# Forgetting attention with a GELU MLP: the last 64 tokens of every batch as a chunk of their own, masking on the matmul engine for the first batch, crossbar transposes merged

## The chip, the cores and the metric

The kernel runs on one core of one Trainium2 chip. The metric is the device time of one execution in microseconds (us); lower is better. The profile is taken on one of these executions; its span, from the first to the last instruction, is about 2 us shorter than the time. All times below are us unless marked ns. PE is the matmul engine (TensorE), ACT is ScalarE, DVE is VectorE, POOL is GpSimd, SP is SyncE, which issues most of the DMAs here.

Runs of one kernel mostly agree within a per cent; a run over 1.5% above the fastest of the same kernel is called slow and left out of ratios.

## The reference

Eight batches, eight heads, 576 tokens, 64 elements per head. Attention with a forget gate, then an MLP with exact GELU (512 to 2048 to 512) over all 4608 tokens:

```python
def _attn_ref(q, k, v, f):
    scores = scale * q @ k.transpose(0, 1, 3, 2)
    cum = np.cumsum(np.log(np.clip(f, 1e-4, 1.0)), axis=-1)
    decay = cum[:, :, :, None] - cum[:, :, None, :]
    scores = np.where(causal, -1e9, scores + decay)   # causal: key after query
    attn = softmax(scores)
    return attn @ v                                   # ... cut: the maximum, the 1e-9
def _moe_ref(x, w_in, w_out):
    h = x @ w_in
    g = 0.5 * h * (1.0 + erf(h / sqrt(2)))
    return g @ w_out
```

The kernel drops the query's part of the decay, which cancels in the softmax, and multiplies the rows of v, and a column of ones, by the key's part ("weighing v").

## The kernel before

Per batch there are four pairs of heads. For each: scores on PE, exp on ACT, the causal mask on POOL, the product with the weighed v ("attend"), normalisation on DVE, and a crossbar transpose (a DMA that transposes on its way) that puts x, the attention's output, into the layout of the MLP. q and k of later batches come by such transposes too, and DVE copies ("untangle") put them in place. Between those pieces PE takes matmuls of the second GEMM of the chunk before (the "fill"). Then the first GEMM of the next chunk of 512 tokens runs in one piece. Chunks are cut from the flat list of 4608 tokens, so chunk c needs x of batch c and, for c above 0, of batches before it. The parts concerned:

```python
def load_v(b, h0=0, h1=H):                       # 5 DMAs on SP
    ...
def x_dma(b, i):                                 # two transposes per pair, on SP
    nc.sync.dma_start_transpose(xT_sb[:, i, q0 : q0 + 512]..., x[:, 0:4]...)
    nc.sync.dma_start_transpose(xT_sb[:, i, q0 + 512 : q0 + S]..., x[D:P, 4]...)

def gemm1(c, ffb):                               # one column block; two tiles of PSUM (where PE writes) in turn
    ps = m_psum.tile([P, TC], FP32, tag="m", name="ps1")
    for kt in range(n_dm):
        nc.tensor.matmul(ps, w_in_sb[...], xT_sb[:, kt, t0 : t0 + TC], ...)
    nc.scalar.activation(g_of[c][ffb], ps, Act.Gelu)

# in gemm2, at the end of a tile of 128 tokens
    nc.vector.tensor_copy(ot, pss[ts])
    nc.sync.dma_start(out[t0 + ts * P : t0 + (ts + 1) * P, :], ot)

for b in range(B):
    if b == 0:
        first_attention()
        load_v(1, 0, 4)
        load_v(1, 4, 8)
    else:
        load_v(b + 1)
        attention(b, gemm2(b - 1, b == 1), ...)
    for ffb in range(n_ff):
        gemm1(b, ffb)
        if b + 1 < B:
            if b == 0 and ffb in (10, 13, 15):   # batch 1: transposes on PE
                transposes_pe(b + 1, ...)
            elif b and ffb % 4 == 0:
                untangle(b + 1, ffb // 4)        # later batches: by the crossbar
            if ffb % 4 == 2:
                weigh_v(b + 1, ffb // 4)         # POOL
            if b == 0 and ffb == 2:
                load_w_out()
    if 0 < b < B - 2:
        load_qk_tokens(b + 2)
```

The softmax here doesn't subtract the row's maximum and nothing guards it: scores larger than these inputs give would overflow.

## Time and profile before

| what | before |
|---|---|
| time, median of the first 3 runs (range) | 377.45 (375.12 to 378.51) |
| span of the profiled run | 374.1 |
| first GEMM of chunk 0 starts | 33.4 |
| first attend of batch 1 | 59.45 |
| last gelu of the first GEMM of chunk 1 starts | 98.13 |
| one undisturbed batch (attention and first GEMM) | 37.7, PE busy for 37.5 |
| last matmul ends, to end of span | 370.4, 3.7 |

The line before the last is the bound: in an undisturbed batch PE hardly rests. What can be won lies at the beginning (loads), at the seams of batches (waits for x) and behind the last matmul. For the end, here is the last output tile of the kernel before: first its DVE copy and its DMA (columns: start, duration, engine and line, what; in brackets the idle time before it and who ended it), then the DMA's own row (KB, us from issue to landing).

```profile
370.39 0.69 DVE L403 COPY ot<-ps 128x512 f32<-128x512 f32 x1 [2.76 <-PE ps L394]
...
371.11 0.33 SPq L404 DMA_DIRECT2D out_dram<-ot  x1
...
out_dram<-ot SPq DMA_DIRECT2D x1, 256.0 KB, 2.0
```

A tile of 128 rows, 256 KB, lands 2.0 after its issue.

### The profile page before, as it was taken

What the parts mean: (1) busy time and instruction counts of PE and PEld (TensorE: products, weight loads), DVE (VectorE), ACT (ScalarE), POOL (GpSimd) and SP (SyncE); (2) the same over time, 40 slices, a digit from 0 to 9 for tenths busy, and PEclk for the clock granted to TensorE, in tenths of its full rate; (3) what the DMA queues carried; (4) which work ended last, traced back from release to release, by engine and by line L of the source; (5) the groups of instructions that cost most, each with busy time, mean ns of one, the idle gap of its engine ahead of it and who ended that gap; (6) DMA issues with size and microseconds to landing.
All of it is one profiled execution on the core that took longest, in us unless ns stands there. A gap on an engine that the chain in (4) does not pass through costs nothing.

```text
span 374.1 us, 6875 instructions
## 1 busy us (share of the span) xinstructions
PE 342.8 (92%) x2665; PEld 185.4 (50%) x2665; DVE 171.5 (46%) x420; ACT 214.0 (57%) x293; POOL 131.1 (35%) x261
## 2 busy tenths in 40 slices
PE   2858949969999699999999999999999999999995
PEld 1545526624465245644564456445654565444442
DVE  6395385548034932477246723681459142011011
ACT  4656647506874378737872688179826882611610
POOL 6578236351155404470447044703560350000000
PEclk9999978999999999999999999999999999999999
DMA  7999999767986894459644976498540023002002
GB/s 110 181 204 184 196 212 162 107 131 138 212 146 87 144 219 109 100 126 210 137 100 119 193 120 106 132 193 140 108 117 2 28 50 102 0 30 84 0 30 84
DMA packets 111057, 45.37 MB, mean 121 GB/s; under 512 B 89968, under 2 KB 106352, under 8 KB 111024
## 3 DMA queue, kind: packets, MB, share of 16 engines
q1 hardware_dynamic: 94128, 31.30, 40.7%
q0 software_dynamic: 16896, 13.63, 24.2%
q8 instruction: 21, 0.34, 0.4%
q14 instruction: 12, 0.10, 0.1%
HBM read 37.90 MB, written 9.44 MB: 127 GB/s over the span
## 4 chain that ended last, share of the span: by engine, by line
PE 77%; ACT 8%; DVE 7%; DMA 3%; SPq 2%; issue 1%; DVEq 0%; ACTq 0%
PE ps L362 33%; PE ps L394 26%; PE s L284 10%; PE o L315 7%; ACT e L294 5%; DMA xT_sb<-x 3%; ACT L294 2%; DVE vw L269 1%; ACT g L374 1%; SPq L350 1%; DVE x L329 1%; DVE ot L403 1%; DMA f_sb<-in_f_dram 1%; SPq L404 1%; DVE qB L183 1%
## 5 line engine op out<-in xcount | busy, mean ns | idle before, releaser
L374 ACT ACTIVATE g<-ps 128x512 bf16<-128x512 f32 x144 | 86.0, 597 | 111.0 <-PE ps L362 111.0
L394 PE MATMUL ps<-w_out_sb,g 128*128 128x512 bf16 x576 | 144.7, 379 | 0.0
L362 PE MATMUL ps<-xT_sb,w_in_sb 128*128 128x512 bf16 x576 | 127.2, 379 | 7.9 <-DMA xT_sb<-x 7.9
L294 ACT ACTIVATE e<-s 128x1024 bf16<-128x1024 f32 (+2 forms) x128 | 103.5, 861 | 25.5 <-PE s L284 24.9
L296 POOL TENSOR_SCALAR_AFFINE_SELECT e<-e 128x256 bf16<-128x256 bf16 x160 | 62.5, 407 | 140.0 <-ACT e L294 138.8
L362 PEld LDWEIGHTS <-w_in_sb 128*128 128x128 bf16 x576 | 56.1, 98 | 76.5 <-issue 10.3
L403 DVE COPY ot<-ps 128x512 f32<-128x512 f32 x36 | 24.9, 692 | 125.7 <-PE ps L394 124.8
L394 PEld LDWEIGHTS <-g 128*128 128x128 bf16 x576 | 50.3, 98 | 41.0
L284 PE MATMUL s<-qA,kT 128*128 128x384 bf16 (+2 forms) x192 | 54.8, 293 | 9.6 <-ACT e L294 4.2
L284 PEld LDWEIGHTS <-kT 128*128 128x128 bf16 x384 | 37.6, 100 | 46.6 <-issue 11.9
L284 PE MATMUL s<-qB,kT 128*128 128x384 bf16 (+2 forms) x192 | 50.3, 294 | 0.3 <-DVE qB L183 0.3
L269 POOL TENSOR_TENSOR vw<-v,wT 128x640 bf16<-128x640 f32 x30 | 38.8, 1292 | 27.6 <-PE o L315 18.5
L315 PE MATMUL o<-vw,e 128*128 128x65 bf16 x960 | 43.6, 194 | 1.6 <-DVE vw L275 1.4
L315 PEld LDWEIGHTS <-e 128*128 128x128 bf16 x960 | 40.4, 98 | 9.1 <-issue 1.4
L328 DVE RECIPROCAL r<-o 128x5 f32<-128x5 f32 x64 | 12.4, 193 | 48.0 <-PE o L315 47.1
L252 DVE COPY kT<-tk 64x288 bf16<-64x288 bf16 x96 | 32.2, 336 | 1.4
L329 DVE TENSOR_TENSOR x<-o,r 128x320 bf16<-128x320 f32 x64 | 31.5, 492 | 2.2
L252 DVE COPY qA<-tq 64x288 bf16<-64x288 bf16 x48 | 20.8, 433 | 0.9
L252 DVE COPY qB<-tq 64x288 bf16<-64x288 bf16 x48 | 16.7, 348 | 0.7
L98 POOL DMA_DIRECT2D q<-in_q_dram x12 | 9.1, 756 | 9.0 <-DMA tq<-q 7.9
L294 ACT ACT_TABLE_LOAD x7 | 9.0, 1283 | 3.3 <-PE s L284 3.2
L374 ACT ACT_TABLE_LOAD x8 | 10.3, 1283 | 0.1
(52 smaller groups left out, 88.5 us busy)
## 6 DMA issues: line engine op xcount, KB each, us to landing
out_dram<-ot SPq DMA_DIRECT2D x36, 256.0 KB, 2.3
v<-in_v_dram SPq DMA_DIRECT2D x30, 256.0 KB, 9.3
q<-in_q_dram POOLq DMA_DIRECT2D x6, 576.0 KB, 7.5
k<-in_k_dram POOLq DMA_DIRECT2D x6, 576.0 KB, 10.7
v<-in_v_dram SPq DMA_DIRECT2D x20, 128.0 KB, 5.3
w_in_sb<-in_moe_w_in_dram POOLq DMA_DIRECT2D x4, 512.0 KB, 10.2
w_out_sb<-in_moe_w_out_dram POOLq DMA_DIRECT2D x4, 512.0 KB, 13.6
xT_sb<-x SPq DMA_TRANSPOSE x56, 2.4
```

The lines of the kernel that those rows point to most:

```text
L252: nc.vector.tensor_copy(rows[:, odd], src[odd * D : (odd + 1) * D, 2 * i + h].rearrange("d j p -> d p j"),)
L269: eng.tensor_tensor(vw_of[b][:, hs, :, 0:D], v_of[b][:, hs, :, :], w.unsqueeze(3).to_broadcast([P, 2, NBLK, D]), Alu.mult,)
L284: nc.tensor.matmul(st[:, h, c : c + w], kT[i][:, K0[n] : K0[n] + P], qt[:, q0 : q0 + w], start=True, stop=True,)
L294: nc.scalar.activation(et[:, :, 0:c], st[:, :, 0:c], Act.Exp, scale=scale)
L296: nc.gpsimd.affine_select(out=et[:, :, c0 : c0 + P], in_=et[:, :, c0 : c0 + P], compare_op=Alu.is_ge, fill=0.0, base=0, pattern=[[0, 2], [ ...
L315: nc.tensor.matmul(o[:, m, :], e_of[b, i, t][:, h, c : c + P], vw_of[b][:, 2 * i + h, n, :], start=(n == 0), stop=(n == m),)
L328: nc.vector.reciprocal(r, o[:, :, D])
L329: nc.vector.tensor_tensor(x_of[b, i][:, :, h, :], o[:, :, 0:D], r.unsqueeze(2).to_broadcast([P, NBLK, D]), Alu.mult,)
L362: nc.tensor.matmul(ps, w_in_sb[:, kt, ffb * P : (ffb + 1) * P], xT_sb[:, kt, t0 : t0 + TC], start=(kt == 0), stop=(kt == n_dm - 1),)
L374: nc.scalar.activation(g_of[c][ffb], ps, Act.Gelu)
L394: nc.tensor.matmul(pss[ts], g_of[c][kt][:, ts * P : (ts + 1) * P], w_out_sb[:, kt, :], start=(kt == 0), stop=(kt == n_ff - 1),)
L403: nc.vector.tensor_copy(ot, pss[ts])
```

## The change

Its intent: keep PE from waiting at the seams. Each batch's first 512 tokens become a chunk, and the 64 last tokens of all eight batches ("tails") become the ninth. So no chunk waits on two batches, one x transpose per pair is enough, and one transpose per batch does the tails. The transposes of q and k are merged (four heads each), and batch 1 gets its q and k by crossbar instead of by PE. In batch 0 the mask becomes a matmul that adds -1e9 to the scores, which relieves POOL. The first two column blocks of each first GEMM run together, all but the last contraction step first (the "pairing"), to hide a late x. The order of the loads is changed: q and k of batch 1 go out between the quarters of w_in instead of behind them, w_out follows at once, and v of batch 1 waits, by a tiny POOL copy (the "gate"), for the last quarter of w_in. The later q and k have two buffers, and from batch 3 on they are loaded behind the first of the four weighings of v instead of behind the last. The last tile is stored in two column parts, from two queues.

```diff
-    qk_pool = ctx.enter_context(tc.tile_pool(name="qk", bufs=1))
+    qk_pool = ctx.enter_context(tc.tile_pool(name="qk", bufs=2))
 # ... cut: buffers, v_sb as one tile, warm-up matmuls, mask constant
-    def transposes_pe(b, i, in_s=True):
-        # ... cut
-    def transpose_dma(b, i):
+    def transpose_dma(b, h0, h1):
 # in scores
-                    stop=True,
+                    stop=b > 0 or c not in SDIAG[t],
+            if b == 0 and c in SDIAG[t]:
+                for h in range(2):
+                    nc.tensor.matmul(
+                        st[:, h, c : c + P], ident_bf, after, start=False, stop=True
+                    )
-        for c0 in SDIAG[t]:
+        for c0 in SDIAG[t] if b else []:
 # tails
+    def x_tail_dma(b):
+        nc.sync.dma_start_transpose(
+            tails[:, :, b * TL : (b + 1) * TL],
+            xt_of[b][D:P].rearrange("p i h d -> p (i h d)"),
+        )
 # gemm1
-    def gemm1(c, ffb):
+    def gemm1(c, ffbs):
+        src = xT(c) if c < B else tails
+        pss = [m_psum.tile([P, TC], FP32, tag="m", name="ps1") for _ in ffbs]
+        for kts in (range(n_dm - 1), [n_dm - 1]):
+            for ffb, ps in zip(ffbs, pss):
+                for kt in kts:
+                    nc.tensor.matmul(ps, w_in_sb[...], src[:, kt, :], ...)
+        for ffb, ps in zip(ffbs, pss):
+            nc.scalar.activation(g_of[c][ffb], ps, Act.Gelu)
 # gemm2
+        if c == B:
+            order[-n_ff:] = [
+                (n_sub - 1, kt, part)
+                for part in ((0, 3 * P), (3 * P, d_model))
+                for kt in range(n_ff)
+            ]
-                nc.sync.dma_start(out[t0 + ts * P : t0 + (ts + 1) * P, :], ot)
+                queue = nc.scalar if c0 else nc.sync
+                if c < B:
+                    rows = out[c * S + ts * P : c * S + (ts + 1) * P, :]
+                else:
+                    n = P // TL
+                    rows = out.rearrange("(b s) d -> b s d", s=S)[
+                        n * ts : n * (ts + 1), TC:S, c0:c1
+                    ]
+                queue.dma_start(rows, ot[:, c0:c1])
 # end of first_attention
+        transpose_dma(1, 0, 4)
 # main loop
+        gemm1(b, (0, 1))
+        if b == 0:
+            for c in range(4):
+                load_w_out(c)
+            nc.gpsimd.tensor_copy(                     # the gate
+                v_sb[0:1, 0:4, 0, 0:1],
+                w_in_sb[0:1, 0, d_ff - 4 : d_ff].unsqueeze(2),
+            )
+            load_v(1, 0, 4)
+            transpose_dma(1, 4, 8)
+            load_v(1, 4, 8)
+            x_tail_dma(0)
+        for ffb in range(2, n_ff):
+            if b + 1 < B:
+                if ffb in (2, 5, 8, 11):
+                    untangle(b + 1, (ffb - 2) // 3)
+                if ffb in (2, 6, 10, 14):
+                    weigh_v(b + 1, ffb // 4)
+            if ffb == 4:
+                load_qk_tokens(b + 2)
+            gemm1(b, (ffb,))
```

## The prediction

> **What bounds the kernel now.** I read the table of stages first (busy time in windows cut at the stage borders of the chain of waits), then the waits of the matmul engine, then the queue that issues DMAs, then the DMA queues. All times are microseconds of the profiled run, span 374.1; the median of the timed runs is 377.45, so I multiply spans by 377.45/374.1 = 1.009.
>
> In the table of stages the columns are window, length, busy time of PE, PE weight loads, DVE, ACT, POOL, then granted clock, DMA share, GB/s. The rows are first attention, first GEMM of chunk 0, attention of batch 1, its first GEMM, attention of batch 2, and an undisturbed attention (batch 3) with its first GEMM:
>
> ```profile
> 0.00:33.40 33.40, 20.07 (x290) 14.66 (x291) 23.77 (x47) 19.45 (x23) 23.47 (x49) 1.00 0.98 167
> 33.40:51.47 18.07, 15.42 (x102) 7.72 (x100) 8.16 (x18) 9.55 (x16) 8.99 (x13) 1.00 1.25 197
> 51.47:84.77 33.30, 27.17 (x248) 16.07 (x249) 19.25 (x47) 15.74 (x18) 14.96 (x31) 0.90 0.83 143
> 98.13:125.70 27.57, 24.36 (x235) 14.30 (x234) 11.20 (x26) 16.05 (x19) 15.03 (x30) 1.00 0.78 136
> 139.06:162.81 23.75, 23.56 (x233) 14.11 (x232) 7.48 (x19) 16.05 (x19) 11.20 (x25) 1.00 0.54 112
> 162.81:176.74 13.93, 13.93 (x66) 6.27 (x65) 12.45 (x33) 8.96 (x16) 3.95 (x6) 1.00 0.99 175
> ```
>
> A batch in the middle is 23.75 + 13.93 = 37.7 and PE is busy all of it; 13.93 for 64 matmuls of 512 columns is 217 ns each. Nothing in the change shortens that work. What can be won is what lies above it: 33.4 of first attention, 18.1 - 13.9 = 4.1 in the first GEMM, 33.3 - 23.7 = 9.6 in batch 1, and waits for the transposed attention output in later batches:
>
> ```profile
> PE ps L362 <- DMA xT_sb<-x: 7.9, 5, 3.6
> POOL vw L269 <- DMA v<-in_v_dram: 8.6, 1, 8.6
> ```
>
> First line: PE waits five times, 7.9 in all, for the crossbar transpose of x (3.6 in batch 1; by windows 0.2 + 2.8 in batch 2, 0.5 and 0.8 in batches 4 and 5). Second: GpSimd waits 8.6 for v of batch 1, until 48.66. The issuing queue in batch 2 shows why x is late:
>
> ```profile
> 112.85 1.26 SPq L238 DMA_TRANSPOSE tq<-q  x1
> 114.16 2.55 SPq L238 DMA_TRANSPOSE tk<-k  x1
> 116.81 1.21 SPq L346 DMA_TRANSPOSE xT_sb<-x  x1
> 118.06 1.23 SPq L350 DMA_TRANSPOSE xT_sb<-x  x1
> ```
>
> Each transpose holds the queue some 1.25, whether it moves 4 blocks (L346) or a 64-row remainder (L350). Sixteen of them per batch are 20 of issue, and the last x goes out behind that.
>
> During the load phase the DMA engines are the bound (share 0.98 and 1.25 in the first two stages). Packets and MB per queue in three windows of 2 us (13 to 15, 29 to 31, 39 to 41); q0 carries casting loads of q, k and weights, q1 v, transposes and stores:
>
> ```profile
> q1 hardware_dynamic: 1471, 0.36, 81.2%
> ...
> q1 hardware_dynamic: 1473, 0.37, 81.2%
> ...
> q0 software_dynamic: 385, 0.29, 91.4%
> q1 hardware_dynamic: 385, 0.09, 36.3%
> ```
>
> Alone v moves 736 packets of 256 B per us; beside weights it gets one packet for each of theirs, here 192 per us. Weights alone make 208 per us (416 in 25 to 27). This decides my prediction.
>
> **What the Trainium skill says.** "DMA: Bandwidth & Descriptors", section "Queues, rings and completion order": each DMA engine round-robins between queue rows at packet granularity. The 385 against 385 agrees. "TensorE: Matmul & The Clock Gate", "Architectural detail": ScalarE, VectorE and GpSimd run their instructions strictly in order; I rest the GpSimd argument on it, and the trace shows no reordering. Same page, Part 1: PE runs at half clock until it has been busy about 3.4 us, and falls back after such an idle time. The trace agrees, though its clock column says 1.00: the 384-column score matmul took 0.50 at 8.27 and 0.32 at 19.42. Same page, "Back-to-back issue gap": about N/2.4 + 2.5 ns, 216 at 512 columns; the 217 above agrees.
>
> **The change part by part.**
>
> First attention. Masking on PE takes 20 affine_selects (407 ns, 8.1) off GpSimd for 40 matmuls of 128 columns (about 56 ns by the skill's gap, 2.2 of PE time with slack beside ACT). Weighing v leaves DVE (1.95 each plus casts, twice). Thirteen warm-up matmuls fill PE before q and k land at 5.6. What is left is ACT: per pair of heads four exps, 1.02 + 0.91 + 1.02 + 0.49 = 3.45, four pairs 13.8. Exps start near 9.3 (9.78 before) and with about 2 of small gaps end near 25.5; then two attends (0.5 each), two normalisations (0.8 each), transposes and copy: 4. First GEMM starts near 29.5 instead of 33.3: -3.8.
>
> First GEMM of chunk 0. The 48 PE transposes of batch 1 and their DVE copies (0.48 each, PE waits 2.6 on the last) go to the crossbar: 18.1 becomes 13.9 + 0.6 of the pairing cost below, -3.6. Scores of batch 1 can start near 44 instead of 51.5.
>
> Pairing in the first GEMM. The first two column blocks now run three contraction steps each before the fourth. That hides 0.65 more of a late x, but block 0 ends later. With two accumulators, block 2 needs block 0's gelu finished. Matmul start to gelu start is 0.41 (from the undisturbed case: first matmul 162.65, fourth 163.30, gelu 163.71), gelu 0.60, release 0.04. Block 1 first waits for the last output copy, which ends 0.89 after the GEMM start: 0.93 + 0.65 = 1.58 for block 0's fourth step, 1.58 + 0.41 + 0.60 + 0.04 = 2.63 for block 2, against 1.80 before. So 0.83 lost per GEMM, eight of them from batch 1 on: +6.6.
>
> Merged transposes. Per batch 16 become 4 + 1 + 4 = 9, 11 of issue instead of 20, and q, k are loaded a batch earlier with two buffers. The queue keeps up and the 7.9 vanish: -7.9. With the pairing, batches 2 to 7 come out even: -4.3 against +5.0.
>
> End. The last tile's copy (0.69) shrinks to 128 columns after the last matmul, its store is smaller: -0.4.
>
> Batch 1, where I expect the gain to be given back. GpSimd's order in the changed program is: weigh v0 and load weights, then four w_out loads, a copy gated on the last w_in quarter, weigh v1 pair 0, load q and k of batch 2, weigh pairs 1 to 3, and only then the masks of batch 1. So the first attend of batch 1 waits for all of v1. In packets (w quarter 512, q and k of a batch 1536, v of a batch 4608): first v half lands near 14.8, weigh to 16.3, w_in flows from 18.3 (issue to flow was 2 before); 512 + 512 weights at 208 per us, 768 of q1, k1 at about 180, 1024 weights: 32.4, landed and gate open 33.4, v1 flowing at 35. By then w_out is queued. First half of v1, 2304 packets: 300 beside the rest of q1, k1, the other 2000 beside w_out at 160 per us (41 to 47 before): 49.1. The crossbar transposes of the second half of batch 1 are next in the same queue: 2304 packets at 1.25 ns, 2.9, to 52.0. Then v1's second half: alone until q2 flows (issued 51.7, flowing 53.7), 1360 packets, the other 944 at 188 per us: 58.7, landed 59.5. Two weighings 3.0, four masks 1.6: first attend at 64.2. Before it was at 59.45. So +4.7 in place of the 7.4 won ahead of it. PE, idle for 14, restarts at half clock for some 3: +1.4.
>
> Sum: 4.7 + 1.4 - 7.9 + 6.6 - 0.4 = +4.4, span 378.5, time 382.
>
> **Rivals.** First, v1 in time: if the loads are not in each other's way as I reckon, the first attend comes near 50, limited by the exps (gelu end, table load, 3.45 for pair 0). Then -9.4 - 7.9 + 6.6 - 0.4 = -11.1, span 363, time 366. For it: the change gates v on w_in on purpose, retunes the fill of batch 1, and looks measured. Against it: the 8.6 wait for v exists already with v issued earlier, and the packet counts. Second, q2 loses the race: v1's second half runs alone behind the transposes, 52.0 + 2.9 + 0.8, weighing and masks to about 60. Then no loss and no gain in batch 1, +0.5 - 7.9 + 6.6 - 0.4 = -1.2, span 373, time 376. Third, pairing costs nothing because x still lands late: then the 7.9 stay in part and the 6.6 overlap them; batches 2 to 7 move by under 2 either way.
>
> **Range and chances.** I give the first rival 0.35, because a tuned change that reorders loads this deliberately was probably seen to work, the second 0.3, my own sum 0.35: 0.35 x 366 + 0.3 x 376 + 0.35 x 382 = 375. Range 363 to 384. The 2% borders are 369.9 and 385: faster 0.33, within 0.57, slower 0.10.
>
> **What would show it.** Right: PE's longest wait is in batch 1, on the masks or weighed v, with GpSimd waiting for v until 50 to 60; the first GEMM of chunk 0 starts at 28 to 31 and takes 14.5; waits of PE for the x transpose vanish; a new wait of about 0.6 on gelu, once per first GEMM, beside 0.3 on the output copy; undisturbed batches near 38.5 instead of 37.7. Wrong: attend in batch 1 before 52 (then the first rival), a first attention above 32, or waits for w_in in chunk 0.

## The result, and the profile after

The changed kernel is slower: 400.06 median of 4 runs (399.90 to 407.81; the last is a slow run) against 377.07 of 4 runs of the kernel before on the same chip. The ratio is 1.0612, 95% interval 1.0551 to 1.0673. (A ratio is the mean time of one kernel's fast runs over that of the other's of the same rounds, so not quite the ratio of the medians quoted.) The spans are 398.2 and 374.1: 24.1 more. Where they arose, by the borders of the stages:

| stretch | before | after | more | predicted |
|---|---|---|---|---|
| start to the last gelu of the first GEMM of chunk 1 | 98.13 | 108.59 | +10.5 | +3.3 |
| six batches, to the last gelu of the first GEMM of chunk 7 | 230.7 | 231.9 | +1.2 | +0.7 |
| last chunk, to the end of its matmuls | 41.5 | 42.7 | +1.2 | +0.8 |
| last matmul to the end | 3.7 | 15.0 | +11.3 | -0.4 |

The last column divides the prediction's own sum of +4.4 over the stretches (in the first, 4.7 + 1.4 + 0.83 of one pairing - 3.6 of the x wait of batch 1; in the second, six pairings less the other x waits). The middle is as predicted. Two places hold nearly everything, and they are read from the following views.

**The beginning.** The waits of PE, then the wait of POOL for v, in the kernel after (columns: total, times, longest):

```profile
PE o L310 <- POOL e L291: 13.8, 2, 13.4
PE s L274 <- DVE kT L243: 4.5, 1, 4.5
...
PE ps L376 <- ACT g L384: 4.3, 9, 0.5
...
POOL vw L259 <- DMA v_sb<-in_v_dram: 32.7, 3, 18.3
```

PE waits 13.4 for the first mask of batch 1 and 4.5 for its transposed k. The 7.9 of waits for x are gone from the list; in their place stand nine waits of 0.5 for gelu. The mask waits behind the weighings of v, and those for v. POOL's timeline shows how long:

```profile
37.23 0.18 POOL L544 CAST v_sb<-w_in_sb 1x4 f32<-1x4 bf16 x1 [7.52 <-DMA w_in_sb<-in_moe_w_in_dram]
55.71 1.27 POOL L259 TENSOR_TENSOR vw<-v_sb,wT 128x640 bf16<-128x640 f32 x1 [18.29 <-DMA v_sb<-in_v_dram]
...
67.69 1.28 POOL L259 TENSOR_TENSOR vw<-v_sb,wT 128x640 bf16<-128x640 f32 x1 [7.36 <-DMA v_sb<-in_v_dram]
...
70.43 1.84 POOL L291 TENSOR_SCALAR_AFFINE_SELECT e<-e 128x256 bf16<-128x256 bf16 x5
```

The gate opens at 37.2, the first half of v is weighed at 55.7, the second at 67.7, and the masks start at 70.4; the first attend follows at 70.89. The SP queue says what shared the way:

```profile
27.24 2.31 SPq L229 DMA_TRANSPOSE tq<-q  x1
29.65 7.79 SPq L229 DMA_TRANSPOSE tk<-k  x1
37.53 12.87 SPq L114 DMA_DIRECT2D v_sb<-in_v_dram  x5
50.51 3.78 SPq L229 DMA_TRANSPOSE tq<-q  x1
54.38 1.32 SPq L229 DMA_TRANSPOSE tk<-k  x1
55.76 3.15 SPq L114 DMA_DIRECT2D v_sb<-in_v_dram  x5
```

A merged transpose can be issued in 1.3 and five loads of v in 3.2, as the last two lines show. Where the queue is crowded the same issues took 7.8 and 12.9. Packets per queue in two windows of 2 us, 33 to 35 and 45 to 47:

```profile
q0 software_dynamic: 349, 0.28, 89.0%
q1 hardware_dynamic: 348, 0.09, 34.4%
...
q0 software_dynamic: 319, 0.31, 91.6%
q1 hardware_dynamic: 320, 0.08, 30.4%
```

In both windows q1 (transposes in the first, v in the second) gets one packet for each packet of q0 (w_in, q, k, w_out). That is the arbitration the prediction quoted from the Trainium skill, "DMA: Bandwidth & Descriptors", section "Queues, rings and completion order"; this trace agrees again, 349 against 348.

**The end.** First the stores of the last chunk on SP and the small one on ACT's queue, then the DMA engines' busy tenths and queues in the window 384 to 396:

```profile
373.56 10.05 SPq L428 DMA_DIRECT2D out_dram<-ot  x4
...
383.56 1.14 ACTq L428 DMA_DIRECT2D out_dram<-ot  x1
```

```profile
DMA  1111111111111111111111111111111111111111
...
q1 hardware_dynamic: 288, 0.53, 11.5%
q10 hardware_dynamic: 130, 0.07, 1.8%
```

PE has finished at 383.2, yet data flow until about 397, in this window never faster than a steady one tenth of the DMA engines: 11.5% + 1.8% = 13.3%, near 2 of 16 (12.5%), 0.60 MB in 12 us, which is 50 KB per us. The chunk's 1 MB of stores, the first of them issued at 373.6, needs 21 at that rate. The Trainium skill states the reason on a page the prediction had cited: "DMA: Bandwidth & Descriptors", section "Why a DMA increments its semaphore by 16 and not by 1". A DMA takes as many engines (up to 16) as divide the slowest dimension of both sides that isn't 1. The DRAM side of these stores is 2 batches by 64 rows, so the slowest dimension is 2. The share agrees with two engines; e1 below tests it.

### The profile page after: what moved, and what is told of

Read it like the earlier page. It is cut to its first block, busy times and chain, and to the rows that moved or that the text cites. A ratio compares the mean times of both kernels' runs of the same rounds, so it can differ in the third digit from the quotient of the medians.

```text
span 398.2 us, 6918 instructions
## 1 busy us (share of the span) xinstructions
PE 349.2 (88%) x2682; PEld 186.4 (47%) x2682; DVE 183.2 (46%) x482; ACT 213.7 (54%) x294; POOL 126.0 (32%) x248
## 4 chain that ended last, share of the span: by engine, by line
PE 64%; SPq 9%; DMA 8%; ACT 8%; POOL 2%; issue 2%; DVE 2%; POOLq 0%; ACTq 0%
PE ps L376 26%; PE ps L410 23%; PE s L274 8%; PE o L310 6%; SPq L114 6%; ACT e L289 4%; SPq L229 4%; DMA v_sb<-in_v_dram 3%; DMA xT<-x 3%; ACT g L384 2%; DMA q<-in_q_dram 2%; ACT L289 2%; DVE ot L419 1%; POOL vw L259 1%; POOL k L102 0%
## 5 line engine op out<-in xcount | busy, mean ns | idle before, releaser
L410 PE MATMUL ps<-w_out_sb,g 128*128 128x512 bf16 (+2 forms) x592 | 145.5, 375 | 0.0
L376 PE MATMUL ps<-xT,w_in_sb 128*128 128x512 bf16 x512 | 114.7, 379 | 4.9 <-ACT g L384 3.8
L291 POOL TENSOR_SCALAR_AFFINE_SELECT e<-e 128x256 bf16<-128x256 bf16 x140 | 54.6, 406 | 133.6 <-ACT e L289 132.6
L376 PEld LDWEIGHTS <-w_in_sb 128*128 128x128 bf16 x576 | 56.1, 97 | 77.1 <-issue 12.4
L419 DVE COPY ot<-ps 128x512 f32<-128x512 f32 (+2 forms) x37 | 25.1, 677 | 110.5 <-PE ps L410 110.3
L274 PE MATMUL s<-qA,kT 128*128 128x384 bf16 (+2 forms) x192 | 54.7, 290 | 10.2 <-DVE kT L243 4.5
L259 POOL TENSOR_TENSOR vw<-v_sb,wT 128x640 bf16<-128x640 f32 x32 | 41.3, 1289 | 50.7 <-DMA v_sb<-in_v_dram 32.7
L243 DVE COPY kT<-tk 64x288 bf16<-64x288 bf16 x112 | 36.4, 325 | 7.7 <-DMA tk<-k 6.1
L325 DVE RECIPROCAL r<-o 128x5 f32<-128x5 f32 x64 | 12.4, 194 | 52.3 <-PE o L310 50.5
L326 DVE TENSOR_TENSOR x<-o,r 128x256 bf16<-128x256 f32 x64 | 27.2, 425 | 2.2
L243 DVE COPY qB<-tq 64x288 bf16<-64x288 bf16 x56 | 24.7, 440 | 0.8
L332 DVE TENSOR_SCALAR xt<-o,r 64x64 bf16<-64x64 f32 x64 | 18.6, 291 | 1.4
L376 PE MATMUL ps<-tails,w_in_sb 128*128 128x512 bf16 x64 | 14.5, 377 | 0.7 <-ACT g L384 0.5
## 6 DMA issues: line engine op xcount, KB each, us to landing
k<-in_k_dram POOLq DMA_DIRECT2D x6, 576.0 KB, 10.5
```

What stands on the lines that cost most here:

```text
L243: nc.vector.tensor_copy(rows[:, odd], src[odd * D : (odd + 1) * D, 2 * i + h].rearrange("d j p -> d p j"),)
L259: nc.gpsimd.tensor_tensor(vw_of[b][:, hs, :, 0:D], v_sb[:, hs, :, :], w.unsqueeze(3).to_broadcast([P, 2, NBLK, D]), Alu.mult,)
L274: nc.tensor.matmul(st[:, h, c : c + w], kT[i][:, K0[n] : K0[n] + P], qt[:, q0 : q0 + w], start=True, stop=b > 0 or c not in SDIAG[t],)
L291: nc.gpsimd.affine_select(out=et[:, :, c0 : c0 + P], in_=et[:, :, c0 : c0 + P], compare_op=Alu.is_ge, fill=0.0, base=0, pattern=[[0, 2], [ ...
L326: nc.vector.tensor_tensor(x_of[b, i][:, :, h, :], o[:, 0:4, 0:D], r[:, 0:4].unsqueeze(2).to_broadcast([P, NBLK - 1, D]), Alu.mult,)
L376: nc.tensor.matmul(ps, w_in_sb[:, kt, ffb * P : (ffb + 1) * P], src[:, kt, :], start=(kt == 0), stop=(kt == n_dm - 1),)
```

## The experiments

The labels are those of the runs. "Whole-row stores" and so on are built on the changed kernel unless said otherwise. All gave correct results. Medians and ratios to the kernel before (376.6 to 377.9):

| run | median | ratio, 95% interval | span |
|---|---|---|---|
| e1_store_halves | 390.21 | 1.0330 (1.0270 to 1.0391) | 387.7 |
| e2_no_column_split | 400.88 | 1.0612 (1.0551 to 1.0673) | 398.5 |
| e3_q2_late | 397.90 | 1.0550 (1.0480 to 1.0620) | 395.4 |
| e4_w_out_q2_late | 393.65 | 1.0389 (1.0314 to 1.0465) | 392.9 |
| e9_transposes_behind_v | 399.84 (one run) | | 398.1 |
| b1_pair (on the kernel before) | 381.38 | 1.0123 (1.0059 to 1.0186) | 379.7 |
| e5_single | 388.31 | 1.0277 (1.0189 to 1.0365) | 385.6 |
| e7_single_qk_late | 377.48 | 1.0006 (0.9960 to 1.0053) | 374.8 |
| e8_pair_qk_late | 383.50 | 1.0143 (1.0091 to 1.0196) | 381.5 |
| best2 | 375.58 | 0.9969 (0.9911 to 1.0027) | 376.4 |
| best3 | 377.02 | 0.9860 (0.9775 to 0.9946), from two fast runs of four | 378.1, a slow run |
| best4 | 384.83 | 1.0186 (1.0140 to 1.0231) | 385.3 |
| best5 | 373.48 | 0.9914 (0.9874 to 0.9953) | 373.1 |

### The end: the shape of the store, or the split

**e1_store_halves** stores each batch's 64 rows by a DMA of its own, so that the slowest dimension is 64 on both sides. **e2_no_column_split** keeps the 2 by 64 shape and takes the column split and the second queue away.

```diff
 # e1
-                    rows = out.rearrange("(b s) d -> b s d", s=S)[
-                        n * ts : n * (ts + 1), TC:S, c0:c1
-                    ]
-                queue.dma_start(rows, ot[:, c0:c1])
+                    for u in range(P // TL):
+                        r0 = (ts * (P // TL) + u) * S + TC
+                        queue.dma_start(out[r0 : r0 + TL, c0:c1],
+                                        ot[u * TL : (u + 1) * TL, c0:c1])
 # e2
-        if c == B:
+        if False:
             order[-n_ff:] = [ ... ]
```

> The changed kernel with one edit: each store of the last chunk is two DMAs of 64 partitions instead of one whose DRAM side has 2 x 64 rows as outer dims. Theory (2 of the 16 DMA engines carry each of these stores because the outermost dim of the DRAM side is 2): the time from the end of the last matmul to the end of the span falls from 15.0 us to 3 to 4 us, the span from 398.2 to about 387, DMA share while they run rises well above 0.13. Rival (the column split, or the store on the ScalarE queue, makes the end slow): nothing changes, span stays at 398.

> The changed kernel with the column split of the last tile taken out: all stores of the last chunk whole and on the SyncE queue, still 2 x 64 rows as outer dims. Theory of the two engines: four stores of 262 KB at about 51 GB/s are 20.5 us from 373.5 on, so the end stays at 394 to 399. Rival (split or the ScalarE queue to blame): the end falls by about 11 us to 387.

Measured: 387.7 and 398.5 of span, against 398.2. In e1 PE ends at 383.6 and the span 4 later. The window 383 to 387 of e1 has the last stores in it; they land 2.2 after their issue, and the engines' share is up to 26% from the 11.5% seen above:

```profile
q1 hardware_dynamic: 197, 0.24, 26.2%
q10 hardware_dynamic: 160, 0.07, 6.2%
...
out_dram<-ot SPq DMA_DIRECT2D x2, 96.0 KB, 2.2
out_dram<-ot ACTq DMA_DIRECT2D x2, 32.0 KB, 2.2
```

What follows: 10.5 of the 24.1 is the shape of the store's DRAM side. (e1 also doubles the number of stores. That a single store isn't slow as such shows in the kernel before, where one DMA of 256 KB landed in 2.0.) The split and the second queue neither caused nor cure it (e2 differs from the changed kernel by 0.3).

### The beginning: what held v back

**e3_q2_late** loads q and k of batch 2 only after the last weighing of batch 1. **e4_w_out_q2_late** does that too and issues the four loads of w_out only after the first weighing.

```diff
 # e3
-            if ffb == 4:
+            if ffb == (4 if b else 14):
                 load_qk_tokens(b + 2)
 # e4, on e3
-            for c in range(4):
-                load_w_out(c)
             nc.gpsimd.tensor_copy(...)     # the gate
+            if b == 0 and ffb == 2:        # behind weigh_v(1, 0)
+                for c in range(4):
+                    load_w_out(c)
```

> The changed kernel with only the load of q and k of batch 2 moved behind the weighing of the last pair of v of batch 1. Theory (packets of the two DMA queues alternate, so v's second half crawls beside this load, 57 to 67.6 us): v's second half lands at about 60 to 61, the first attend of batch 1 comes at about 64 instead of 70.9, span 398.2 to about 391. Rival (v waits for its own queue, behind crossbar transposes): the attend stays within 2 us of 70.9.

> As e3_q2_late, and the w_out loads too are issued only after the first pair of v of batch 1 is weighed. Theory of alternating packets: with the weight queue empty after q and k of batch 1, the crossbar transposes and v move at 700 to 900 packets per us instead of 160: first weighing at 42 to 45 instead of 55.7, first attend at 53 to 57 instead of 70.9, the wait of PE for the untangled k (4.5 us) shorter, span 398.2 to about 383. Rival (PE, not DMA, sets batch 1, or w_out comes too late): the attend moves but the first GEMM of chunk 1 does not start more than 5 us earlier.

Measured, e3: the second half of v is weighed at 61.06 instead of 67.69, the first attend comes at 66.08 instead of 70.89, the span falls by 2.8, less than half of the 7 expected. Measured, e4 (POOL, then PE):

```profile
44.00 1.40 POOL L259 TENSOR_TENSOR vw<-v_sb,wT 128x640 bf16<-128x640 f32 x1 [8.85 <-DMA v_sb<-in_v_dram]
...
56.59 1.28 POOL L259 TENSOR_TENSOR vw<-v_sb,wT 128x640 bf16<-128x640 f32 x1 [6.35 <-DMA v_sb<-in_v_dram]
```

```profile
53.33 1.01 PE L410 MATMUL ps<-w_out_sb,g 128*128 128x512 bf16 x2 [3.06 <-DMA w_out_sb<-in_moe_w_out_dram]
...
61.41 0.29 PE L310 MATMUL o<-vw,e 128*128 128x65 bf16 x2 [6.33 <-POOL e L291]
```

Without w_out beside it the first half of v is there 11.7 earlier (44.0 against 55.7); w_out then meets the second half instead, which is weighed at 56.6, and PE waits 3.1 for w_out itself. The first GEMM of chunk 1 ends 9.3 earlier than in the changed kernel (last gelu at 99.33), but the span only by 5.3: in batch 2 a load of q and k was issued at 121.12 beside an x transpose at 121.22, and x landed 6.0 after its issue, for which PE waited 2.6. The first weighing came as expected; the first attend, at 61.4, missed 53 to 57, and the span of 392.9 missed 383. The rival that PE sets batch 1 is out. So v does set its start, and with q2 and w_out moved the first attend comes 9.5 earlier, though still 2.0 later than in the kernel before.

**e9_transposes_behind_v** asks about the rest. The prediction counted the packets of v, of the weights, of q and k, and of the transposes of the second half of batch 1. It left out those of the first half, another 2304 packets, which stand ahead of v in the same queue. Here they are issued behind v's first half.

```diff
-        transpose_dma(1, 0, 4)             # at the end of first_attention
...
             load_v(1, 0, 4)
+            transpose_dma(1, 0, 4)
             transpose_dma(1, 4, 8)
             load_v(1, 4, 8)
```

> The changed kernel with the transposes of the first half of batch 1 issued behind the first half of v instead of ahead of it. If their 2304 packets ahead of v are the term that the prediction left out, the gate opens near 33.5 (37.2 in the changed kernel) and the first weighing of batch 1 is near 49 to 51 (55.7), where the prediction had them; the scores of batch 1 then start later, and the second half of v gains nothing. If they are not, gate and first weighing stay within 1 of 37.2 and 55.7.

```profile
33.91 0.18 POOL L543 CAST v_sb<-w_in_sb 1x4 f32<-1x4 bf16 x1 [4.41 <-DMA w_in_sb<-in_moe_w_in_dram]
51.28 1.27 POOL L259 TENSOR_TENSOR vw<-v_sb,wT 128x640 bf16<-128x640 f32 x1 [17.19 <-DMA v_sb<-in_v_dram]
...
66.50 1.28 POOL L259 TENSOR_TENSOR vw<-v_sb,wT 128x640 bf16<-128x640 f32 x1 [10.61 <-DMA v_sb<-in_v_dram]
```

The gate opens at 33.9 (predicted 33.4) and v's first half is weighed at 51.3 (the prediction had it landed at 49.1); in the changed kernel these were 37.2 and 55.7. How far such times move by themselves is seen in e1, e2, e3, e5, e7 and e8, which load the same in the same order up to there: gate 35.1 to 35.8, first weighing 54.7 to 55.6. So of the gate's 3.3 only 1.1 is clear of that scatter, of the weighing's 4.4 at least 3.4. The one run doesn't show the time moving (399.84): the same packets now come ahead of the second half, weighed at 66.5, and PE waits 12.4 for k of batch 1. So the omitted packets are most of what was wrong with the first half of the prediction's chain, 3.4 to 4.4 of the 6.6 between 49.1 and 55.7, and leaving them out was a mistake of counting. The other 2 or so stand in e9 too, where v's packets begin only after 37 and not at 35.

### The middle: pairing, and a late x

**b1_pair** is the kernel before with the pairing and nothing else. **e5_single** is e1 without the pairing.

```diff
 # e5, on e1 (b1_pair is the reverse, on the kernel before)
-        gemm1(b, (0, 1))
+        gemm1(b, (0,))
+        gemm1(b, (1,))
```

> The kernel before with only the pairing of the first two column blocks of each first GEMM. Reckoned: 0.83 us per first GEMM from chunk 1 on and 0.6 in chunk 0 (block 2 waits for the gelu of block 0 and block 1 for the last output copy), up to 0.65 won back in each of the five GEMMs that wait for x: span from 374.1 to between 377 and 381, and waits of PE on gelu of some 0.5 each appear. Rival (pairing costs nothing, x is late anyway): span within 1.5 us of 374.

> The changed kernel with the stores of the last chunk as two DMAs each (as e1_store_halves) and without the pairing. If pairing costs 0.83 in each of nine first GEMMs and x were in time, the span falls by 7 from the 387.7 of e1_store_halves. But x of the last pair landed 1.85 after the GEMM start in batches 3 to 5, so without pairing the wait should show as 1.2 us on the x transpose there: I expect a fall of 2 to 5 us. Rival: no fall, the waits on x take all of it.

On the kernel before, pairing costs 1.2% (381.38, span 379.7, as expected), with nine waits for gelu of 4.2 in all; the waits for x fall from 7.9 to 4.0. On e1, taking it away wins 2.1 of span, and now waits for x appear, which pairing had hidden:

```profile
95.79 13.32 PE L376 MATMUL ps<-xT,w_in_sb 128*128 128x512 bf16 x61 [1.11 <-DMA xT<-x]
134.38 13.33 PE L376 MATMUL ps<-xT,w_in_sb 128*128 128x512 bf16 x61 [0.83 <-DMA xT<-x]
173.07 13.33 PE L376 MATMUL ps<-xT,w_in_sb 128*128 128x512 bf16 x61 [0.93 <-DMA xT<-x]
```

So x is still late in the changed kernel, against the prediction's -7.9, though the queue that issues it keeps up. In its trace the last x of batch 3 is issued at 168.38, and the load of q and k of batch 5 starts on POOL at 168.90, 0.5 later; in the kernel before, that load started at 165.10, 4.4 after the x issued at 160.69. **e7_single_qk_late** moves the load back behind all four weighings in every batch; **e8_pair_qk_late** is e7 with the pairing put back, so that it has no late x to hide.

```diff
 # e7, on e5; e8, on e1
-            if ffb == 4:
+            if ffb == 14:
                 load_qk_tokens(b + 2)
```

> As e5_single, and in every batch the load of q and k two batches ahead is issued only after the four weighings of v instead of after the first. If the late landing of x (4.1 us in place of 2.4) comes from that load starting at the same moment, x lands in 2.5 us again, the waits on x vanish and the span falls by 3 to 8 us more than in e5_single; the part of it that falls in batch 1 is what e3_q2_late showed, about 3. Rival (the tail transpose queued right behind x delays it): x still lands in 4 us in batches 3 to 5.

> The 377.5 version with the pairing of the first two column blocks put back, nothing else. There x arrives in time (0.3 of waits), so the pairing can hide nothing: by the prediction's working it costs 0.83 in each of 8 or 9 first GEMMs, +6.6 to +7.5, about 384 to 385, with a wait of about 0.5 for gelu in each. If the rival holds that pairing is free, 377 to 378.

e7 is 10.8 of span faster than e5, more than expected, and level with the kernel before. About half comes from batch 1, as in e3 (first attend at 65.16 against 70.45), half from x: of 5.2 of waits 0.3 are left. The tail transpose still goes out right behind x, so that rival is out. In e8 the pairing costs 6.7 of span from one profiled run to the other; the ratios, 1.0143 against 1.0006, taken on two chips, make it 5.2. An undisturbed batch shows it: 38.5 from one of the following lines to the next (129.69, 168.21), against 37.7 to 37.9 per batch in e7.

```profile
129.69 12.25 PE L376 MATMUL ps<-xT,w_in_sb 128*128 128x512 bf16 x56 [0.47 <-ACT g L384]
...
168.21 12.25 PE L376 MATMUL ps<-xT,w_in_sb 128*128 128x512 bf16 x56 [0.47 <-ACT g L384]
```

Each line is the 56 matmuls that follow the two paired blocks; the bracket is block 2's wait for block 0's gelu. The rival "pairing costs nothing" holds only where x is late.

### Towards a version that beats both

**best2** takes e7's stores and single blocks, issues v ahead of the transposes, without the gate, and cuts the loads of w_out and the last two weighings into the attention of batch 1.

```diff
+        load_v(1, 0, 4)                    # ungated
         transpose_dma(1, 0, 4)
 # w_out: quarter 0 at once, quarters 1 to 3 between the masks of batch 1
+                    if (i, t) == (0, 3):
+                        load_w_out(1)
+                        weigh_v(1, 2)
+                    elif (i, t) == (1, 1):
+                        load_w_out(2)
+                    elif (i, t) == (1, 3):
+                        weigh_v(1, 3)
+                        load_w_out(3)
+                    elif (i, t) == (2, 1):
+                        load_qk_tokens(2)
```

> All lessons at once: stores in halves, no pairing, v of batch 1 ungated and its first half ahead of the crossbar transposes, w_out in four pieces between the masks of batch 1, weighing of pairs 2 and 3 after the masks of pair 0, q and k of batch 2 last. If the theory of packets and of GpSimd's strict order holds, the first attend of batch 1 comes at 49 to 54, PE does not wait over 2 us there, and the span is 355 to 366, below the kernel before. Rival (first attention and batch 1 have another bound): span above 370.

A miss: 375.58, level with the kernel before. PE gets v sooner (first attend 57.48) but now waits 5.0 for k's transposes, which stand behind v, then 1.8 for w_out, and 7.0 for x in batches 1 and 2: the load of v of batch 2 held the SP queue from 63.6 to 80.4, beside w_out and q2, with x behind it.

**best3** puts the transposes first again, v gated, only one quarter of w_out between v's halves, and v of batch 2 behind the last x of batch 1:

```diff
         transpose_dma(1, 0, 4)
 # gate, then
             load_v(1, 0, 4)
 # w_out: quarter 0 behind weigh_v(1, 0), the others as in best2
 # v of batch 2: at the end of the attention of batch 1
+            load_v(2, 0, 4)
             transpose_dma(2, 0, 4)
+            load_v(2, 4, 8)
             transpose_dma(2, 4, 8)
```

> Aim: beat both kernels. The version with whole-row stores, no pairing and late q and k loads (377.5), plus the loads of batch 1 in the order in which they are needed: transposes of its first half, v first half still gated on w_in, then the first quarter of w_out after the first weighing, v second half; the other quarters of w_out, the weighings of pairs 2 and 3 and q and k of batch 2 go between the masks of batch 1; v of batch 2 goes out after the last x of batch 1. If the account of batch 1 is right (v, not PE, set its start, because of what shared the queues), scores start near 44 and the first attend near 51 instead of 65, the last gelu of the first GEMM of chunk 1 starts at 88 to 92 instead of 102.3, and with 37.8 for every later batch the span is 361 to 366. If moving loads only moves the waits on, as in the version before, x or v of batch 2 is late instead and the span stays at 370 or more.

Batch 1 went as its account said: first attend at 53.97 (51 expected), last gelu of the first GEMM of chunk 1 about 12 earlier than in e7. But the four runs spread from 371.35 to 381.77, two of them fall under slow, the profiled one too. Its trace shows one wait that holds most of the gain, and the span of 361 to 366 wasn't reached by the fast runs either (369.6 and 372.5). SP, POOL and PE in it:

```profile
116.56 1.45 SPq L350 DMA_TRANSPOSE xT<-x  x1
```

```profile
116.53 0.82 POOL L102 DMA_DIRECT2D q<-in_q_dram  x1
```

```profile
127.03 5.28 PE L376 MATMUL ps<-xT,w_in_sb 128*128 128x512 bf16 x12 [9.55 <-DMA xT<-x]
```

POOL, free earlier than in e7, issued q of batch 4 0.03 before the last x of batch 2, and x landed 10.4 later. **best4** moves the load of q and k (from batch 2 on) into the middle of the attention. **best5** leaves it where best3 has it and adds a gate: POOL first copies four elements of the last transposed x into the q buffer.

```diff
 # best4, on best3
+                if b > 1 and (i, t) == (2, 0):
+                    load_qk_tokens(b + 2)
 # best5, on best3
+                    nc.gpsimd.tensor_copy(
+                        qk_of[b + 2][0][0:1, 0, 0:4], xT(b)[0:1, HP - 1, TC - 4 : TC]
+                    )
                 load_qk_tokens(b + 2)
```

> The version before (377.0 median, two fast runs at 371 and 374) with one thing moved: from batch 2 on, q and k of the batch after next are loaded in the middle of the attention (behind the masks of its pair 2) and not after the weighings. There the load was queued at 116.53, 0.03 before the last x of batch 2 at 116.56, and that x landed 10.4 later and PE waited 9.6. If the collision of that load with x is what makes x late, the wait goes and the span is 361 to 365, time 363 to 367, faster than both kernels by 2.5 to 4%. If the stall belongs to the chip's state or to something else in batch 2, a wait of several us for x stays and the span is 368 or more.

> The third version (its profiled run 378.1 span, with one wait of 9.6 for the last x of batch 2) with one gate added: GpSimd loads q and k of the batch after next only after it has copied four elements of the last transposed x into the q buffer, so that load can no longer be in the queues together with the last x. If the collision of that load with x is what makes x late, the last x of batch 2 lands within about 2.5 of its issue, no wait for x above 1 is left, and the span is 365 to 369, time 367 to 371. If something else in batch 2 holds x up (v of batch 3, the transposes of batch 3, the output stores in the same queue), a wait of several us stays there and the time is as in the third version, 374 to 380.

best4 missed, by turning one collision into another. In its batch 2 q and k (105.75) met v of batch 3 (104.67), whose issue then held SP for 11, and the next output store got out only behind it and two transposes, at 121.68; the copy of a later output tile was done at 126.7, and PE waited for it:

```profile
104.67 11.06 SPq L114 DMA_DIRECT2D v_sb<-in_v_dram  x5
...
121.68 0.74 SPq L423 DMA_DIRECT2D out_dram<-ot  x1
```

```profile
126.72 1.01 PE L376 MATMUL ps<-xT,w_in_sb 128*128 128x512 bf16 x2 [8.58 <-DVE ot L419]
```

best5 is half a hit: all six runs between 372.70 and 374.81, ratio 0.9914, so 0.9% faster than the kernel before (within the 2% that counts as the same) and 6.6% faster than the changed kernel (0.9914 / 1.0612). The wait of 9.6 is gone; four waits for x are left, 3.7 in all, the longest 1.9 where none above 1 was expected. The time is short of the 367 to 371 expected: in batch 2 PE still loses 5, 2.2 for an output copy and 2.8 for x. A likely reason, read from the trace and not tested: q of batch 3 lands late, and its transposes (the last issued at 112.86) keep the SP queue ahead of x and the stores. That it is the collision of that load which delays x rests on e5 against e7 and on best5's gate; that it also makes best3's slow runs slow is shown for the one run that has a trace, not for the other.

## Why the prediction was wrong

It gave 375, with 0.10 for slower by over 2%; 400 was measured. By its own steps:

- **First attention and first GEMM of chunk 0: right.** The first GEMM started at 30.07 (29.5 predicted, 33.4 before), and its matmuls ran 14.6 (14.5 predicted). What masking on PE and the warm-up each gave wasn't tested apart.
- **Pairing: right.** Nine waits of 0.47 for gelu; 38.5 per undisturbed batch. Alone it measured 5.2 to 6.7 in e8, against 7.2 (+6.6, and 0.6 in chunk 0).
- **Merged transposes, "the 7.9 vanish": half right.** The issue queue kept up, but a new wait took the old one's place. "q, k are loaded a batch earlier" misread the change: they are loaded two batches ahead in both kernels (batch 4 at 124.2 before, at 130.4 after), and what moved is their place behind the weighings, which puts the load at the moment of the last x. e5 shows 5.2 of waits for x where pairing doesn't hide them. In the sum it didn't show, for the pairing hid most of it; the six middle batches came out at +1.2 against +0.7.
- **Batch 1: the mechanism right, a term of the sum left out.** The prediction's own account had POOL waiting for v until 59.5 and the first attend at 64.2; it came at 70.9. The omitted term is the 2304 packets of the transposes of batch 1's first half, counted as a gain on PE and not as a load in v's queue. By e9 they are 3.4 to 4.4 of the 6.6 by which v's first half was late. The second half landed 8.1 late (67.6 instead of 59.5): it went out at 55.8 instead of 52.0, and from 59 to 67 its queue got 146 packets per us beside q and k of batch 2, where the prediction reckoned 188 for the last 944. e3, without that load beside it, has the second half about 6 earlier; how the 8.1 divides between the late start and the slower sharing was not measured. The omitted transposes came late themselves too: scores of batch 1 started at 49.2, not 44, behind a 4.5 wait for k (1.7 to 4.5 in e1, e2, e3, e7 and e8). The restart at half clock came as said: from 70.9 to 74 the granted clock was 0.50, and score matmuls of 320 columns took 0.47 instead of 0.30. In the first stretch this is +10.5 in place of +3.3.
- **The end: the step that failed outright.** "Its store is smaller: -0.4" was +11.3. The prediction looked at the size of the last store and not at its shape: two outer rows in DRAM, two DMA engines of sixteen. e1 gives 10.5 of span back with the same bytes.
- **The mixing of rivals.** The prediction's own sum was 382. It gave 0.35 to "v1 in time", because the change looked deliberately tuned, and that took the number to 375. Nothing in the profile spoke for it; the packet counts spoke against it, and they erred on the other side. (A slip of reading without effect: the text over the table of stages names seven stages and the table has six rows; the first GEMM of batch 1, 84.77 to 98.13, isn't in it.)

The four stretches add up: (10.5 - 3.3) + (1.2 - 0.7) + (1.2 - 0.8) + (11.3 + 0.4) = 19.8, the gap between the predicted span, 378.5, and the measured 398.2.

## What to carry to other kernels

For each DMA that a change touches, write down the outermost dimension of both sides before its size: a regrouped output can put a store on two engines. When a transpose moves from PE to the crossbar, count its packets into the queue where it now stands, ahead of everything behind it. And when an engine that issues loads gets free earlier, ask which transfer its next load will now meet; here a gate on the data that must not be disturbed (best5) did better than another place in the program (best4), though such a move was enough in e7.

## What the Trainium skill lacked or had wrong

- "DMA: Bandwidth & Descriptors", section "Why a DMA increments its semaphore by 16 and not by 1": nothing wrong, but overlooked. What the runs add is the cost: here 2 engines with packets of 2 KB moved 50 KB per us (0.60 MB in 12), and the 128-row store of the same 256 KB landed in 2.0.
- The same page, section "Queues, rings and completion order": the round-robin by packets is right (349 against 348), but it doesn't say what it does to bytes: the queue with small packets got 0.09 MB where the other got 0.28. Nor does it say that an issue can take longer when the queues are crowded: five loads of v took 3.15 to issue in one place and 12.87 in another.
- The same page, section "DMA Transpose (X-bar)": the section has no figure for issuing one. Here it is about 1.2 for four blocks as for a 64-row remainder, and 1.3 for a merged transpose of four heads.
- "TensorE: Matmul & The Clock Gate", section "Back-to-back issue gap": the prediction took its formula, 216 ns at 512 columns. The section calls that the gap of a single matmul and gives about 131 ns for a stream in a real kernel; here 64 in a stream took 217 ns each, so the formula fits and the 131 doesn't.
- The same page, Part 1: the half clock after an idle time is right. In best4 two matmuls of 512 columns took 1.01 behind a wait of 8.6, and in e8 two took 0.59 where PE had been busy. The profile's granted clock doesn't always show it: in the kernel before, a 384-column matmul took 0.50 at 8.27 under a column of 1.00.
